# Key copy of the second pair on GpSimd, its lower part behind the key matches, and its query matches in another PSUM bank

## The chip, the cores and the metric

One core of one Trainium2 chip runs the whole program. The metric is the device time of one execution in microseconds (us), as the median of several runs. The core has TensorE (PE; its weight loads are listed as PEld), VectorE (DVE), ScalarE (ACT), GpSimd (POOL) and SyncE (SP), which here only issues DMAs. Each engine works through its own instructions in a fixed order.

## What is computed

Attention with a hash mask, followed by two feed-forward layers. Each query and key row gets a 6-bit bucket from the signs of its products with `proj`; a query sees only the keys of its own bucket.

```python
mask = q_bucket[:, :, :, None] == k_bucket[:, :, None, :]
scores = np.where(mask, scale * np.matmul(q, k.transpose(0, 1, 3, 2)), -1e9)
attn_out = softmax(scores) @ v                       # 2 batches, 8 heads, 768 rows, 64 wide
x = rearranged attn_out                              # 1536 tokens x 512
x = np.maximum(x @ w_in, 0) ** 2 @ w_out             # layer one, 2048 wide
h = x @ w_in2
return (np.maximum(h, 0) + alpha * np.minimum(h, 0)) @ w_out2   # layer two
```

All results are f32. The kernel gets f32 quality out of TensorE's f32r products by splitting a number into a high part (rounded to f32r) and a low part (the rest) and multiplying the parts.

## The kernel before

The 1536 tokens are cut into four chunks of 384 query rows. `attention_first` computes the attention of the first chunk with nothing beside it. After that `feed_forward` runs layer one for chunk after chunk, with the attention of the next chunk woven in, and then comes layer two.

In a chunk the eight heads are taken as four pairs, `Pair(c, j)`. In this text **pair 0** is `Pair(0, 0)`, **pair 1** is `Pair(0, 1)` (the one that the change touches), and so on. A pair has six **units**: head h = 0 or 1, and three blocks of 128 query rows. Units are counted on over the pairs of the first chunk: units 0 to 5 are pair 0 (3 to 5 its second head), 6 to 11 pair 1, 12 to 17 pair 2.

One unit does this: four products into a PSUM tile of two banks (`scores`, L468; the tiles `s` and `acc` take turns), the row maximum on VectorE (`low`, L476), the exponential on ScalarE (`sm`, L477, which frees the tile), then two units later two groups of three transposes on TensorE (`p_t`, L495, into a bank `m` or `x`) and an eviction of each group by ScalarE or VectorE (`pt`, L500 or L502, by the letters of `EVICT`). Later the products with the values follow (`blocks`, L512, into the bank `h`).

The operands of a unit's four products are stacked: 64 partitions hold the head's own numbers, the other 64 hold the bucket codes and the low parts. For keys, a pair needs in SBUF `kh`, the key rounded to f32r (`k_split`, L327, ScalarE), its low part (L328, VectorE, in place in `kr`), and the code matches (`k_ids`: products with `code`, L306, then L340 on VectorE). Four DMAs of 384 KB each then put them into `k`: for each head one from `kh` (`k_rows`, L334) and one from `kr` (L345). For queries: `q_ids` makes the matches (L314) and `q_yes` turns them into codes on ScalarE (L389, two instructions); `q_halves` makes high and low parts (L369 ScalarE, L370 GpSimd, L371 VectorE).

Pair 0 has its own preparation, `at_once`. For its second head one DMA of 96 KB copies a high part across partitions, `q<-q` (L433); the second of the four products of unit 3 is the first that waits for it, as the program's waits show.

What sets the order. Instructions that are passed to `tc.keep_in_program_order` keep the order in which the code is written; in the first chunk that holds for all of TensorE's and part of the others. The rest is placed by a list scheduler. SyncE's DMAs all go into one hardware queue, in the order in which the scheduler put them. PSUM banks: two for `m`, one `x` (every third `m_tile()`), one `h`, and two pairs for `s` and `acc`. The matches of pair 1's queries take an `m_tile()`, and the bank is free again when `q_yes` has read it.

Of the kernel before, what the change touches and what calls it, by code (L numbers as in the profile page):

```python
# [8 lines left out]
F32R = mybir.dt.float32r  # L9
# [3 lines left out]
AF = mybir.ActivationFunctionType  # L13
ALU = mybir.AluOpType
# [17 lines left out]
def kernel(  # L32
# [20 lines left out]
    nc = tc.nc  # L53
# [49 lines left out]
    def s_tile():  # L103

        state["s"] += 1
        if not state["moe"] and state["s"] % 2 == 0:
            return ps_a.tile([P, 2, 512], F32, tag="acc", name="acc")
        return ps_s.tile([P, 2, 512], F32, tag="s", name="s")

    def m_tile():  # L110

        state["m"] += 1
        if not state["moe"] and state["m"] % 3 == 0:
            return ps_a.tile([P, 512], F32, tag="x", name="x")
        return ps_m.tile([P, 512], F32, tag="m", name="m")

    def h_tile():

        state["h"] += 1
        if not state["attention"] and state["h"] % 3:  # L120
            return ps_m.tile([P, 512], F32, tag="m", name="m")
        return ps_h.tile([P, 512], F32, tag="h", name="h")

    def f32(ap):
        return ap.bitcast(F32)
# [89 lines left out]
    def load_values(b, j):  # L215
        vr = p4.tile([P, NKB, 2 * D], F32, tag="vr", name="vr")
        keys[b, j][-1] = vr
        return nc.sync.dma_start(out=vr, in_=v[b, j])

    class Pair:  # L220
# [78 lines left out]
        def matches(self, bits, n):  # L299

            w = n // NG
            if n > T and self.c == 0 and not self.first:
                halves = [m_tile()[:, 0:T] for _ in range(2)]
                for g in range(NG):
                    a, k = divmod(g * w, T)
                    self.pe(nc.tensor.matmul(halves[a][:, k:k + w], code[:, g, :], bits, start=True, stop=True))  # L306
                return halves
            if n > T:
                ps = s_tile()
            else:  # L310
                ps = m_tile().unsqueeze(1)
            for g in range(NG):
                a, k = divmod(g * w, T)
                self.pe(nc.tensor.matmul(ps[:, a, k:k + w], code[:, g, :], bits, start=True, stop=True))  # L314
            return ps[:, 0:n // T, 0:T]
# [8 lines left out]
        def k_split(self):  # L324
            self.new_k()
            kh = p1.tile([P, S], F32R, tag="kh", name="kh")
            self.next(nc.scalar.activation(kh, self.kr[:, 1], AF.Copy))  # L327
            nc.vector.tensor_tensor(self.kr[:, 1].bitcast(F32R), self.kr[:, 1], f32(kh), ALU.subtract)  # L328
            self.kh = kh
            self.k_rows(0)  # L330

        def k_rows(self, h):
            r, o = self.rows(h)
            nc.sync.dma_start(out=f32(self.k[r, h]), in_=f32(self.kh[r]).unsqueeze(1).to_broadcast([D, 2, S]))  # L334

        def k_ids(self):
            y = self.matches(self.k_code, S)
            ids = self.kr[:, 0].bitcast(F32R).rearrange("p (a n) -> p a n", n=T)
            for x, to in [(y[a], ids[:, a]) for a in range(2)] if self.c == 0 else [(y, ids)]:
                nc.vector.tensor_scalar(to, x, pop, -1.0, ALU.not_equal, ALU.mult)  # L340
            for h in range(2):
                r, o = self.rows(h)
                if h:
                    self.k_rows(1)
                ins = nc.sync.dma_start(out=f32(self.k[o, h]), in_=self.kr[r])  # L345
            keyed[self.c, self.j] = ins

            tc.keep_in_program_order(load_values(self.b, self.j))
            self.vr = keys[self.b, self.j][-1]
# [960 lines left out]
```

## Time and profile before

| what | us |
|---|---|
| median of 3 runs | 770.59 (770.19 to 771.94) |
| the profiled execution, its own time | 770.93 |
| its span, first to last instruction | 769.2 |
| time of that execution outside the span | 1.7 |

The profile is one execution. Times in the rows are microseconds from the start of the span. "[1.85 <-ACT q L389]" behind a row says that the engine had been idle for 1.85 us before it, and that the ScalarE instruction of line 389 ended the idle time. A row's second number runs to the end of its last instruction; the next row can start before that, since the engines are pipelined. The granted clock of TensorE is 1.00 of full speed in every row used here.

### The profile page before, as it was taken

Reading aid. Unit: us, or ns where it says so; the run is one execution under the profiler, and the core shown is the slowest. Engines: PE = TensorE matmul, PEld = TensorE weight load, DVE = VectorE, ACT = ScalarE, POOL = GpSimd, SP = SyncE. Lnnn points to the kernel's source line nnn. Section 1 sums busy time; section 2 is a strip of 40 time slices with the busy share of each in tenths; the row PEclk is TensorE's granted clock in tenths of the full one; section 3 lists DMA queues with packets and bytes.
Section 4 is the critical chain, followed back from the end, with each engine's and each line's share of the span. In section 5 each row is a group of like instructions: output and inputs, shape, how many; then the busy total and the mean of one; then the engine's idle time right before and its main releaser. Section 6 shows DMA issues by size and latency. Waiting matters only on the chain. (4 is left out here: it accounts for less than half of the span.)

```text
span 769.2 us, 12401 instructions
## 1 busy us (share of the span) xinstructions
PE 750.9 (98%) x4361; PEld 636.2 (83%) x4361; DVE 536.9 (70%) x950; ACT 510.0 (66%) x990; POOL 141.7 (18%) x89
## 2 busy tenths in 40 slices
PE   7999999999999999999999999999999999999998
PEld 4667877877887878778778789999998889998886
DVE  8878888887886969998888654836665914665111
ACT  8987887876665757767666567757786435876331
POOL 1101000000000000000000000006566535567440
PEclk9999999999999999999999999999999999999999
DMA  6778877978888997788866685332212246311222
GB/s 182 201 189 278 257 239 259 281 224 234 229 265 242 262 267 257 261 302 270 265 237 196 206 278 179 110 117 97 95 52 60 66 139 225 108 66 55 68 56 95
DMA packets 56705, 143.65 MB, mean 187 GB/s; under 512 B 7402, under 2 KB 11652, under 8 KB 56644
## 3 DMA queue, kind: packets, MB, share of 16 engines
q1 hardware_dynamic: 56644, 142.87, 59.6%
q8 instruction: 34, 0.56, 0.3%
q14 instruction: 27, 0.22, 0.1%
HBM read 96.62 MB, written 25.47 MB: 159 GB/s over the span
## 5 line engine op out<-in xcount | busy, mean ns | idle before, releaser
L1028 POOL TENSOR_TENSOR wp<-wraw,wp 128x1024 fp32r<-128x1024 f32 (+1 forms) x30 | 63.7, 2126 | 499.3 <-ACT wp L1025 486.4
L766 DVE TENSOR_TENSOR wl<-wf,wh 128x512 fp32r<-128x512 f32 x128 | 86.6, 686 | 17.8 <-ACT wh L765 17.3
L477 ACT ACTIVATE sm<-s,low 128x768 f32<-128x768 f32 x84 | 75.5, 898 | 28.9 <-DVE low L476 28.8
L765 ACT ACTIVATE wh<-wf 128x512 fp32r<-128x512 f32 x128 | 79.2, 627 | 20.8 <-DMA wf<-w 6.8
L476 DVE TENSOR_REDUCE low<-s 128x1 f32<-128x768 f32 x84 | 80.2, 954 | 16.3 <-PE s L468 15.2
L495 PE MATMUL m<-ident,sm 128*128 128x128 f32 x531 | 82.5, 274 | 2.6 <-ACT q L389 1.8
L468 PE MATMUL s<-k,q 128*128 128x384 f32 x336 | 76.9, 350 | 4.1 <-ACT sm L477 3.9
L495 PEld LDWEIGHTS m<-ident,sm 128*128 128x128 f32 x531 | 65.0, 140 | 18.0 <-ACT q L389 2.1
L1125 PE MATMUL b<-wp,gp 128*128 128x512 f32 x192 | 75.1, 391 | 0.0
L803 PE MATMUL h<-xh,wh 128*128 128x384 f32 x208 | 74.4, 358 | 0.6 <-ACT u L518 0.3
L999 PE MATMUL b<-xph,wp 128*128 128x384 f32 x224 | 74.9, 334 | 0.0
L1000 PE MATMUL b<-xpl,wp 128*128 128x384 f32 x224 | 74.9, 334 | 0.0
L1001 PE MATMUL b<-xph,wp 128*128 128x384 f32 x224 | 74.9, 334 | 0.0
L1126 PE MATMUL b<-wp,gp 128*128 128x512 f32 x192 | 74.8, 390 | 0.0
L1115 POOL TENSOR_TENSOR gp<-g,gp 128x768 fp32r<-128x768 f32 x32 | 62.4, 1954 | 51.3 <-ACT gp L1112 51.2
L468 PEld LDWEIGHTS s<-k,q 128*128 128x128 f32 x336 | 56.9, 188 | 17.7 <-ACT sm L477 11.3
L804 PE MATMUL h<-xl,wh 128*128 128x384 f32 x208 | 70.7, 340 | 0.0
L805 PE MATMUL h<-xh,wl 128*128 128x384 f32 x208 | 70.4, 338 | 0.0
L1109 DVE TENSOR_TENSOR wp<-wp 128x512 fp32r<-128x512 f32 x28 | 26.0, 938 | 62.4 <-ACT wp L1106 59.1
L844 PE MATMUL acc<-wh,gh 128*128 128x512 f32 x144 | 61.9, 431 | 0.0
L502 DVE COPY pt<-m 128x384 f32<-128x384 f32 x99 | 54.0, 550 | 7.1 <-PE m L495 6.8
L845 PE MATMUL acc<-wl,gh 128*128 128x512 f32 x144 | 57.4, 399 | 0.0
(191 smaller groups left out, 1647.7 us busy)
## 6 DMA issues: line engine op xcount, KB each, us to landing
wf<-w SPq DMA_DIRECT2D x96, 256.0 KB, 4.0
wbits<-in_w_in_dram SPq DMA_DIRECT2D x32, 512.0 KB, 4.7
wbits<-in_w_out_dram SPq DMA_DIRECT2D x32, 512.0 KB, 5.6
wraw<-ws SPq DMA_DIRECT2D x16, 896.0 KB, 4.6
q<-q SPq DMA_DIRECT2D x48, 192.0 KB, 4.5
w<-wf SPq DMA_DIRECT2D x32, 256.0 KB, 4.4
wp<-w SPq DMA_DIRECT2D x32, 256.0 KB, 2.6
k<-kh SPq DMA_DIRECT2D x14, 384.0 KB, 7.6
```

What stands on the lines that cost most here:

```text
L468: self.pe(nc.tensor.matmul(ps[:, a, 0:HALF], self.q[:, h, i, qs], self.k[:, h, i, ks], start=i == 0, stop=i == 1))
L476: low_ins = nc.vector.tensor_reduce(low, ps[:, 0:2, 0:HALF], AX.XY, ALU.max, negate=True)
L477: sm_ins = nc.scalar.activation(sm.rearrange("p (a n) -> p a n", a=2), ps[:, 0:2, 0:HALF], AF.Exp, bias=low, accum_out=self.sums[:, i:i + 1],)
L495: self.pe(nc.tensor.transpose(ps[:, i * P:(i + 1) * P], pp[:, b * P:(b + 1) * P], ident))
L765: nc.scalar.activation(hi, w, AF.Copy)
L766: nc.vector.tensor_tensor(lo, w, f32(hi), ALU.subtract)
L803: nc.tensor.matmul(hp, wih[:, ks], xh[:, kk, :], start=first, stop=False)
L999: nc.tensor.matmul(ps, w[0][:, ms], gh, start=first, stop=False, skip_group_check=True)
L1000: nc.tensor.matmul(ps, w[0][:, ms], gl, start=False, stop=False, skip_group_check=True)
L1001: nc.tensor.matmul(ps, w[1][:, ms], gh, start=False, stop=last, skip_group_check=True)
L1125: nc.tensor.matmul(a, g[:, 0, b], w[:, 0], start=f == 0, stop=False)
L1126: nc.tensor.matmul(a, g[:, 0, b], w[:, 1], start=False, stop=False)
```

## The change

Four edits, all in the first chunk. (1) `kh` of pair 1 is copied by GpSimd and no longer by ScalarE. (2) The subtraction that makes the key's low part is a method of its own, `k_low`, and for pair 1 it is written behind the two L340 instructions of `k_ids`. (3) The query matches of pair 1 go to the bank `h` and not to an `m_tile()`; the count of `m_tile()` calls is one lower from there on, so which of the later tiles is `m` and which is `x` shifts. (4) `kh` of pairs 2 and 3 is kept in program order on ScalarE.

```diff
-                ps = m_tile().unsqueeze(1)
+                ps = (h_tile() if (self.c, self.j) == (0, 1) else m_tile()).unsqueeze(1)
...
             kh = p1.tile([P, S], F32R, tag="kh", name="kh")
-            self.next(nc.scalar.activation(kh, self.kr[:, 1], AF.Copy))
-            nc.vector.tensor_tensor(self.kr[:, 1].bitcast(F32R), self.kr[:, 1], f32(kh), ALU.subtract)
             self.kh = kh
+            if (self.c, self.j) == (0, 1):
+                tc.keep_in_program_order(nc.gpsimd.tensor_copy(kh, self.kr[:, 1]))
+            else:
+                ins = nc.scalar.activation(kh, self.kr[:, 1], AF.Copy)
+                if self.c == 0:
+                    tc.keep_in_program_order(ins)
+                self.k_low()
             self.k_rows(0)
+
+        def k_low(self):
+            nc.vector.tensor_tensor(self.kr[:, 1].bitcast(F32R), self.kr[:, 1], f32(self.kh), ALU.subtract)
...
                 nc.vector.tensor_scalar(to, x, pop, -1.0, ALU.not_equal, ALU.mult)
+            if (self.c, self.j) == (0, 1):
+                self.k_low()
```

Line numbers of the changed kernel are 4 to 10 higher from here on. The scheduler also places other things anew. Below are three places in the two programs, with buffer numbers.

SyncE's queue, from the first DMA that pair 0's preparation issues; `kh_255` and `k_254` are pair 1's, `kr_216` its raw keys, `kr_229` and `qn_231` the loads for pair 2, `q_175` pair 0's queries. Before:

```order
L403 DMA k_174<-k_174 64x768
L200 DMA kr_229<-in_kT_dram 128x768
L433 DMA q_175<-q_175 64x384
L206 DMA qn_231<-in_qT_dram 128x384
L334 DMA k_254<-kh_255 64x2x768
L345 DMA k_254<-kr_216 64x1536
L334 DMA k_254<-kh_255 64x2x768
L345 DMA k_254<-kr_216 64x1536
```

And in the changed kernel:

```order
L413 DMA k_174<-k_174 64x768
L342 DMA k_254<-kh_255 64x2x768 x2
L200 DMA kr_229<-in_kT_dram 128x768
L443 DMA q_175<-q_175 64x384
L206 DMA qn_231<-in_qT_dram 128x384
L355 DMA k_254<-kr_216 64x1536 x2
```

Both DMAs from `kh_255` now stand ahead of the loads for pair 2 and of `q_175<-q_175`.

ScalarE, from behind the exponential of unit 1 (`sm_278`, `sm_306`, `sm_331` are units 2, 3 and 4; `m_290` and `m_295` or `x_295` are the transposes of unit 0, `m_320` the second group of unit 1, `q_286` is pair 1's). Before:

```order
L327 ACTIVATE kh_255<-kr_216 128x768
L500 ACTIVATE pt_289<-m_290 128x384
L500 ACTIVATE pt_289<-x_295 128x384
L477 ACTIVATE sm_278,sums_173<-acc_272,low_277 128x768
L389 ACTIVATE q_286<-m_281,off_114 64x384 x2
L477 ACTIVATE sm_306,sums_173<-s_300,low_305 128x768
L369 ACTIVATE q_286<-qn_218 64x384 x2
L500 ACTIVATE pt_289<-m_320 128x384
L500 ACTIVATE pt_289<-x_334 128x384
```

And in the changed kernel:

```order
L510 ACTIVATE pt_289<-m_290 128x384
L510 ACTIVATE pt_289<-m_295 128x384
L510 ACTIVATE pt_289<-m_320 128x384
L487 ACTIVATE sm_278,sums_173<-acc_272,low_277 128x768
L399 ACTIVATE q_286<-h_281,off_114 64x384 x2
L487 ACTIVATE sm_306,sums_173<-s_300,low_305 128x768
L379 ACTIVATE q_286<-qn_218 64x384 x2
L487 ACTIVATE sm_331,sums_173<-acc_325,low_330 128x768
L510 ACTIVATE pt_289<-m_334 128x384
```

The key copy is gone, and the eviction of unit 1's second group has moved ahead of the exponential of unit 2.

TensorE, from the last product of pair 1's query matches (tile 281) on. Before:

```order
L314 MATMUL m_281<-bits_243,code_111 128x96
L495 MATMUL m_290<-ident_108,sm_226 128x128 x3
L495 MATMUL x_295<-ident_108,sm_226 128x128 x3
L468 MATMUL s_300<-k_174,q_175 128x384 x4
L495 MATMUL m_315<-ident_108,sm_251 128x128 x3
L495 MATMUL m_320<-ident_108,sm_251 128x128 x3
L468 MATMUL acc_325<-k_174,q_175 128x384 x4
```

And in the changed kernel:

```order
L314 MATMUL h_281<-bits_243,code_111 128x96
L505 MATMUL m_290<-ident_108,sm_226 128x128 x3
L505 MATMUL m_295<-ident_108,sm_226 128x128 x3
L478 MATMUL s_300<-k_174,q_175 128x384 x4
L505 MATMUL x_315<-ident_108,sm_251 128x128 x3
L505 MATMUL m_320<-ident_108,sm_251 128x128 x3
L478 MATMUL acc_325<-k_174,q_175 128x384 x4
```

The sequence is the same; the banks differ. Unit 3 (`s_300`) stands ahead of both groups of unit 1 in both programs. Further down the queue, the loads of two weight blocks (`wbits`, 512 KB each), which stood behind all of pair 3's key rows, now stand ahead of pair 2's.

## Rows read from the trace of the kernel before

**Rows 1.** Busy time by stretch: window, its length, then us per engine, clock, DMA

```profile
10.00:18.00 8.00, 5.98 (x42) 4.80 (x41) 6.11 (x9) 7.41 (x15) 0.46 (x1) 1.00 0.64 157
24.00:36.00 12.00, 11.91 (x85) 8.18 (x86) 10.39 (x19) 10.58 (x24) 1.61 (x2) 1.00 0.83 207
36.00:60.00 24.00, 23.60 (x170) 17.28 (x171) 19.06 (x32) 20.80 (x45) 1.69 (x2) 1.00 0.66 184
```

**Rows 2.** Timeline of TensorE: start, us, what; units 3, 6, 9, 12, transposes

```profile
13.00 0.94 PE L468 MATMUL s<-k,q 128*128 128x384 f32 x4
...
16.11 0.55 PE L495 MATMUL m<-ident,sm 128*128 128x128 f32 x3 [1.85 <-ACT q L389]
...
19.99 0.97 PE L468 MATMUL acc<-k,q 128*128 128x384 f32 x4 [0.47 <-ACT sm L477]
...
25.80 0.49 PE L495 MATMUL x<-ident,sm 128*128 128x128 f32 x3
26.20 0.96 PE L468 MATMUL s<-k,q 128*128 128x384 f32 x4
...
35.04 0.94 PE L468 MATMUL acc<-k,q 128*128 128x384 f32 x4
```

**Rows 3.** Timeline of ScalarE from the key copy to the exponential of unit 7

```profile
12.39 0.83 ACT L327 ACTIVATE kh<-kr 128x768 fp32r<-128x768 f32 x1
...
13.49 0.49 ACT L500 ACTIVATE pt<-x 128x384 f32<-128x384 f32 x1
13.86 0.91 ACT L477 ACTIVATE sm<-acc,low 128x768 f32<-128x768 f32 x1
...
14.89 1.17 ACT L389 ACTIVATE q<-m,off 64x384 fp32r<-64x384 f32 x2
16.08 0.90 ACT L477 ACTIVATE sm<-s,low 128x768 f32<-128x768 f32 x1
...
16.97 1.05 ACT L369 ACTIVATE q<-qn 64x384 fp32r<-64x384 f32 x2
...
18.94 0.90 ACT L477 ACTIVATE sm<-acc,low 128x768 f32<-128x768 f32 x1
...
25.16 0.89 ACT L477 ACTIVATE sm<-s,low 128x768 f32<-128x768 f32 x1
```

**Rows 4.** Timeline of SyncE's DMA issues: start, us that the issue took

```profile
3.57 0.44 SPq L200 DMA_DIRECT2D kr<-in_kT_dram  x1
...
8.81 0.47 SPq L433 DMA_DIRECT2D q<-q  x1
9.39 0.53 SPq L206 DMA_DIRECT2D qn<-in_qT_dram  x1
13.25 0.66 SPq L334 DMA_DIRECT2D k<-kh  x1
...
25.29 0.62 SPq L334 DMA_DIRECT2D k<-kh  x1
```

**Rows 5.** GpSimd: two casts of the timeline, and a group of the page

```profile
4.78 0.82 POOL L402 CAST k<-k 64x768 fp32r<-64x768 f32 x1 [3.44 <-ACT k L401]
6.26 0.67 POOL L405 CAST q<-q 64x384 fp32r<-64x384 f32 x1 [0.67 <-ACT q L404]
...
L1115 POOL TENSOR_TENSOR gp<-g,gp 128x768 fp32r<-128x768 f32 x32 | 62.4, 1954 | 51.3 <-ACT gp L1112 51.2
```

**Rows 6.** Stretches again; the last two numbers are DMA share and GB/s

```profile
12.00:13.00 1.00, 1.00 (x12) 0.67 (x9) 1.00 (x3) 1.00 (x3) 0.00 (x0) 1.00 0.09 29
14.00:15.00 1.00, 0.26 (x3) 0.02 (x1) 1.00 (x2) 0.98 (x3) 0.00 (x0) 1.00 0.42 89
14.50:24.20 9.70, 7.31 (x60) 6.03 (x61) 7.53 (x12) 9.48 (x22) 2.40 (x4) 1.00 0.94 221
```

**Rows 7.** DMA issues of the first 10 us: KB, then us from issue to landing

```profile
qn<-in_qT_dram SPq DMA_DIRECT2D x3, 192.0 KB, 3.5
vr<-in_v_dram SPq DMA_DIRECT2D x1, 384.0 KB, 4.4
```

## The prediction

> **What bounds the kernel now.** I read the stretches first, then TensorE's timeline where it is idle, then the timelines of the engines that end that idle time, and last SyncE's issues and the DMA table. The stretches [rows 1] show two regimes. From 24 to 36 us TensorE is busy 11.91 of 12.00 us, and from 36 to 60 us 23.60 of 24.00: whatever TensorE has lost by 24 us, it can make up less than half a microsecond of before 60. From 10 to 18 us it is busy 5.98 of 8.00, while ScalarE is busy 7.41: here TensorE waits and ScalarE sets the pace. The largest idle time of that stretch is one row [rows 2]: the transposes at 16.11 us had 1.85 us of idle time ahead of them, ended by L389, `q_yes`. These transposes (second group of unit 1) wanted the bank that held pair 1's query matches, and `q_yes` stood in ScalarE's row behind the key copy, two evictions and an exponential [rows 3]. The change aims at this place, so the question is how early TensorE reaches unit 9 (26.20 us before [rows 2]), from where its row is full. A shift there is a shift of the end.
>
> **The change, part by part.** *Removed.* The key copy leaves ScalarE: 0.83 us at 12.39 us [rows 3]. The bank wait goes, 1.85 us on TensorE [rows 2], because the matches now sit in `h`, which the order shows unused until the values' products. If nothing else were late, TensorE would gain at most these 1.85 us.
>
> *Added on GpSimd.* One cast of 128x768. The trace has no such cast; below it is 64x768 in 0.82 us, above it 128x768 with two inputs in 1.95 us [rows 5]. I take 0.82, the same operation of the same length per partition. It starts when pair 1's raw keys have landed. They were issued at 3.57 us [rows 4]; a load of the same size landed 4.4 us after its issue [rows 7], so at 8.0. The copy ends at about 8.9.
>
> *Moved on SyncE.* This is the part that decides. Both DMAs from `kh`, 384 KB each, now stand in SyncE's row ahead of the key load for pair 2 (384 KB) and of `q<-q` (96 KB), and they wait for GpSimd. Before, `q<-q` was issued at 8.81 us [rows 4] and had landed by 12.9, since the query load issued behind it at 9.39 landed 3.5 us later [rows 4, 7]; unit 3, which needs it, ran at 13.00 without any wait [rows 2]. Now the first `kh` DMA is issued at 9.0, the second 0.66 later [rows 4], the load after that, and `q<-q` at about 10.9. Its bytes stand behind 1152 KB. The bytes of a DMA into an empty queue begin about 1.3 us after the issue: the one issued at 13.25 [rows 4] gives the second from 14 to 15 a DMA share of 0.42 [rows 6], so from 14.6 on. That puts the first bytes at 10.3. The full queue moved 221 GB/s from 14.5 to 24.2 us, mostly with these same copies [rows 6]: 1248 KB are 1.28 MB, 5.8 us, to 16.1. Landing comes some 0.8 us after the bytes: the load that landed at 12.9 left only a share of 0.09 in the second from 12 to 13 [rows 6], so its bytes were over at 12.1. **`q<-q` lands at 16.9 us**, and unit 3's second product waits for it, where it ran at 13.2 before.
>
> *What is queued behind that wait.* TensorE keeps its order, so both transpose groups of unit 1 wait with unit 3. On ScalarE the eviction of the second group now stands ahead of the exponential of unit 2, so ScalarE stops too. From the landing: three products, 0.6 us until the next group can start; one group later the second starts, 0.40 us (25.80 to 26.20 [rows 2]), and ends 0.49 later: 18.4. ScalarE evicts (0.37 until the next, 13.49 to 13.86 [rows 3]): 18.8. Exponential of unit 2, 1.03 (13.86 to 14.89): 19.8. `q_yes`, 1.19 (14.89 to 16.08): 21.0. Exponential of unit 3, 0.89 (16.08 to 16.97): 21.9. The two L369, 1.05: 22.9. Exponential of unit 4 at 22.9, against 18.94 before [rows 3]. It frees the tile for unit 6 after 0.9 us, as before (19.99, idle time ended by `sm` [rows 2]): unit 6 at 23.9, 3.9 us late. From unit 4's to unit 7's exponential ScalarE needed 6.22 us (18.94 to 25.16 [rows 3]); it now has one eviction more in between and 0.2 us of idle time less, so the shift stays at 3.9 to 4.1 up to unit 9. Written as a rule: the shift is the landing of `q<-q` minus 12.9.
>
> *Beside it at no cost.* `k_low` now precedes the maximum of unit 2 on VectorE: 0.9 us later for a maximum that ScalarE asks for at 18.8, so the wait hides it; without the wait it would cost ScalarE most of that. Pair 1's own key rows: two of four DMAs are early, the other two follow `q<-q` and the query load, 1.0 MB more, 4.5 us at 221 GB/s, landing at about 21, ahead of unit 6 at 23.9. The two weight loads of 512 KB ahead of pair 2's key rows are 4.7 us of queue. Before, pair 2's first key row was issued at 25.29 and its first unit ran at 35.04 [rows 2, 4], 9.7 us later, and needs 768 KB, 1.3 + 3.6 + 0.8 = 5.7 us. So 4.0 us are free, and the loads start before the rows, which wait for ScalarE. I take 0, and 0.7 as the upper end. The kept order of `kh` for pairs 2 and 3 and the shifted bank names change places in a row where TensorE is full: 0, within 0.5 either way.
>
> *Sum.* Landing 16.9 minus 12.9 gives 4.0, less 0.1 for the little slack up to 60 us: +3.9 us on the profiled execution's 770.93 is 774.8. The median of the runs is 0.34 below that execution, so 770.59 + 3.9 = 774.5 us.
>
> **Rivals.** *A: the bank wait goes and nothing comes in its place.* If `q<-q` still landed by 12.9, TensorE would lose no time at unit 3, and up to 1.85 us would be won: 768.7. For it speaks that ScalarE has one copy less in a stretch where it is the bound [rows 1]. Against it, `q<-q` is issued behind a DMA that cannot be issued before 9.0; it decides the other way only if 96 KB land within 2 us of an issue at 10.9, and the shortest landing in [rows 7] is 3.5.
>
> *B: only the later issue counts.* If the 16 DMA engines let the small transfer end with little regard to the copies ahead of it, it lands 3.5 us after its issue [rows 7]: 14.4, and the shift is 1.5: 772.1, at the border of what counts as no change. For it: its bytes are a thirteenth of the queue's. Against it: the DMA share is 0.94 over ten microseconds of such copies [rows 6], so a later transfer finds no idle engine. The Trainium skill ("DMA: Bandwidth & Descriptors", Anatomy of one DMA) gives 2.0 us plus the bytes at 436 GB/s for one DMA, on another issue path; by that the landing would be an estimated 13.9 and the time 771.6. The trace does not agree: 221 GB/s in a full queue [rows 6].
>
> *C: GpSimd is slow.* At 1.95 us [rows 5] the copy ends at 10.0 and everything behind is 1.1 later: 775.6, and with 0.7 for the weight loads 776.3. For it: the half as long 64x384 cast took 0.67 against 0.82 [rows 5], so a cast can be slower than its length says. The Trainium skill ("SBUF — State Buffer", Who interferes with whom) has GpSimd and a VectorE instruction with two SBUF inputs block each other entirely, and pair 0's preparation has such subtractions on VectorE at that time; no row here settles it.
>
> That the change does not do what it says is out: the order shows each of the moves.
>
> **How the numbers follow.** Forecast 0.66 at 774.5; A 0.07 at 768.7; B 0.14 at 772.1, of which I put 0.08 within no change; C 0.13 at 775.6 to 776.3. What can be told from no change here is about 0.2%, 1.5 us, so the borders are 769.1 and 772.1. Faster 0.07; within 0.2% 0.09, which is B's part and a little for a forecast that later idle time eats; slower 0.84. The forecast's own bounds are a landing between 15.5 and 17.9 us, +2.6 to +5.0, 773.2 to 775.6. The range reaches to B below, 771.9, and to C above, 776.3; it leaves out A and the tails.
>
> **What would show it.** In the profile of the changed kernel: a gap of 3 us or more in TensorE's row in the middle of unit 3, ended by a DMA `q<-q`; SyncE's row with two `k<-kh` issues from about 9.0 on and `q<-q` behind them near 11; ScalarE idle from about 13.7 to 18 in front of its third eviction; no wait for L399 any more; unit 6 at about 23.9 and unit 9 at about 30. I am wrong if unit 3 runs near 13 without a wait, which makes A true, or if the wait is there but unit 12 is no later than about 36, which would mean that the full row had slack after all.

## The result

The changed kernel takes 774.82 us (median of 22 runs) beside 771.23 us for the kernel before (22 runs in the same session): ratio 1.0053, with a 95% interval from 1.0034 to 1.0071. A second set of runs of the same file gave 775.50 us, ratio 1.0076 (1.0048 to 1.0105). It is slower by about half a per cent, near the forecast of 774.5 us. The profiled execution took 773.33 us, 1.5 us less than the median of its runs; its span is 771.5.

**Stretches** of the changed kernel, in the columns of [rows 1]: window, its length, busy time of TensorE, weight load, VectorE, ScalarE, GpSimd, then granted clock, DMA share and GB/s.

```profile
10.00:18.00 8.00, 5.45 (x41) 4.21 (x41) 5.32 (x8) 3.16 (x7) 0.00 (x0) 1.00 0.86 212
24.00:36.00 12.00, 11.08 (x87) 7.99 (x87) 11.02 (x19) 10.87 (x23) 1.51 (x3) 1.00 0.71 197
21.00:22.00 1.00, 1.00 (x4) 1.00 (x5) 0.00 (x0) 0.96 (x3) 0.00 (x0) 0.50 0.91 289
22.00:23.00 1.00, 1.00 (x6) 0.90 (x5) 0.50 (x1) 1.00 (x3) 0.00 (x0) 0.50 0.09 26
```

From 10 to 18 us ScalarE is busy 3.16 us where it was busy 7.41 [rows 1]: it no longer sets the pace there, it stands still. TensorE is not faster for that, 5.45 us against 5.98. From 24 to 36 us TensorE has 0.92 us of idle time, where it had 0.09: the full row of [rows 1] begins later. The last two rows hold something that [rows 1] has nowhere: a granted clock of 0.50, the 1.2 GHz level, while TensorE is full again.

**SyncE's issues**, which answer [rows 4], and the new cast on GpSimd. The two stretches behind them show when the bytes begin: the DMA share is the last number but one.

```profile
9.69 1.30 SPq L342 DMA_DIRECT2D k<-kh  x2
11.09 1.43 SPq L200 DMA_DIRECT2D kr<-in_kT_dram  x1
12.62 1.58 SPq L443 DMA_DIRECT2D q<-q  x1
```

```profile
8.84 0.82 POOL L329 CAST kh<-kr 128x768 fp32r<-128x768 f32 x1 [1.92 <-DMA kr<-in_kT_dram]
```

```profile
10.00:11.00 1.00, 1.00 (x17) 0.60 (x16) 0.96 (x2) 0.30 (x1) 0.00 (x0) 1.00 0.01 3
11.00:12.00 1.00, 1.00 (x11) 0.88 (x4) 0.52 (x2) 0.90 (x2) 0.00 (x0) 1.00 0.95 194
```

The order is the one that was read from the code: both copies from `kh`, the key load of pair 2, then `q<-q`. GpSimd's cast took the 0.82 us that were taken for it, but the raw keys landed only when it started, at 8.8 us instead of 8.0.

**TensorE**, which answers [rows 2]: units 3, 4, 6, 9 and 12 (start, duration, in brackets the idle time ahead and what ended it).

```profile
14.89 0.42 PE L478 MATMUL s<-k,q 128*128 128x384 f32 x1
17.86 0.77 PE L478 MATMUL s<-k,q 128*128 128x384 f32 x3 [2.55 <-DMA q<-q]
...
20.75 1.65 PE L478 MATMUL acc<-k,q 128*128 128x384 f32 x4 [1.46 <-ACT sm L487]
...
25.31 0.55 PE L505 MATMUL m<-ident,sm 128*128 128x128 f32 x3 [0.48 <-ACT pt L510]
25.61 0.95 PE L478 MATMUL acc<-k,q 128*128 128x384 f32 x4
...
31.95 0.97 PE L478 MATMUL s<-k,q 128*128 128x384 f32 x4
...
40.80 0.95 PE L478 MATMUL acc<-k,q 128*128 128x384 f32 x4
```

The first product of unit 3 runs, then 2.55 us pass until `q<-q` is there. The wait for L389 of [rows 2] is gone, and no wait for L399, which took its place, has come.

**ScalarE**, which answers [rows 3]:

```profile
14.84 0.87 ACT L510 ACTIVATE pt<-m 128x384 f32<-128x384 f32 x2
19.32 0.49 ACT L510 ACTIVATE pt<-m 128x384 f32<-128x384 f32 x1 [3.61 <-PE m L505]
19.71 0.90 ACT L487 ACTIVATE sm<-acc,low 128x768 f32<-128x768 f32 x1
...
20.72 1.16 ACT L399 ACTIVATE q<-h,off 64x384 fp32r<-64x384 f32 x2
21.91 0.90 ACT L487 ACTIVATE sm<-s,low 128x768 f32<-128x768 f32 x1
...
23.88 0.90 ACT L487 ACTIVATE sm<-acc,low 128x768 f32<-128x768 f32 x1
```

It stands idle for 3.61 us in front of its third eviction, and then needs 4.56 us from there to the exponential of unit 4 (19.32 to 23.88), much as the prediction's chain had it (18.4 to 22.9).

### The profile page after: what moved, and what is told of

Its sections match the earlier page's. It is cut to its first block, busy times and chain, and to the rows that moved or that the text cites. A ratio compares the mean times of both kernels' runs of the same rounds, so it can differ in the third digit from the quotient of the medians.

```text
span 771.5 us, 12403 instructions
## 1 busy us (share of the span) xinstructions
PE 753.7 (98%) x4361; PEld 639.0 (83%) x4361; DVE 537.5 (70%) x950; ACT 507.6 (66%) x989; POOL 142.5 (18%) x90
## 4 chain that ended last, share of the span: by engine, by line
PE 87%; DMA 6%; DVE 3%; ACT 3%; issue 1%; SPq 1%; ACTq 0%; DVEq 0%
PE s L478 7%; PE m L505 6%; PE b L1135 6%; PE b L1136 6%; PE m L522 5%; PE b L1141 5%; PE b L1011 5%; PE b L1010 5%; PE b L1009 5%; PE h L813 4%; PE h L814 4%; PE h L815 4%; PE acc L858 4%; PE acc L855 3%; PE acc L854 3%; PE h L522 2%
## 5 line engine op out<-in xcount | busy, mean ns | idle before, releaser
L478 PE MATMUL s<-k,q 128*128 128x384 f32 x336 | 78.5, 354 | 5.8 <-DMA q<-q 2.5
```

Of the source, the lines that this page charges most:

```text
L478: self.pe(nc.tensor.matmul(ps[:, a, 0:HALF], self.q[:, h, i, qs], self.k[:, h, i, ks], start=i == 0, stop=i == 1))
```

## A second look at both kernels

By the two first profiles, unit 6 is 5.62 us late (25.61 against 19.99 [rows 2]), while the spans are only 2.4 apart (771.5 and 769.2). So I first believed that layer one gives some 3 us back. To test that, both kernels were run again, without an edit.

> The changed kernel as it is, on the same chip as the three others. Ratio 1.0034 to 1.0071 as in its first comparison. In its trace: unit 3's wait ended by q<-q between 15.5 and 17.9 us, unit 6 at 23.9 to 25.6. It also tells whether the 3.4 us at half clock behind that wait, and the late rise of the clock to full speed at 13.6 us, come again.

Measured: 775.50 us, ratio 1.0076, a little above the expected range; unit 3's second product at 17.28 us, 3.00 us of idle time ahead, unit 6 at 25.35, span 771.6. Stretches at a granted clock of 0.50 came again, in other places: from 8.12 to 11.53 us and from 18.36 to 25.19.

> The kernel before, unchanged: a second profiled execution of it, and a measure of how far a comparison of a kernel with itself strays. All theories: ratio 1.000 with an interval that holds 1.000; a stretch at half clock of under 4 us in all; unit 6 within 0.5 us of 20, layer one's first product within 1 us of 71.7. Open: whether the time from layer one's first product to the end is 697.5 us again, as in the first profile. Theory 1 (the changed kernel gives 2 to 3 us back behind layer one's start): 697 to 698. Rival (that time varies from run to run, and the first profile of before was a long one): 693 to 696.

Measured: 771.38 us, ratio 1.0003 (0.9986 to 1.0019), so a comparison of a kernel with itself strays by up to 0.19%. Unit 6 and layer one's first product came 2.3 us later than in the first profile, which no theory expected. TensorE in this second profile of the kernel before, the first unit to be compared, then units 3, 4, 6 and 12:

```profile
8.43 1.65 PE L468 MATMUL acc<-k,q 128*128 128x384 f32 x4 [0.66 <-ACT q L422]
...
15.31 0.95 PE L468 MATMUL s<-k,q 128*128 128x384 f32 x4
...
18.42 0.55 PE L495 MATMUL m<-ident,sm 128*128 128x128 f32 x3 [1.84 <-ACT q L389]
...
22.31 0.97 PE L468 MATMUL acc<-k,q 128*128 128x384 f32 x4 [0.47 <-ACT sm L477]
...
37.36 0.94 PE L468 MATMUL acc<-k,q 128*128 128x384 f32 x4
...
74.00 0.44 PE L803 MATMUL h<-xh,wh 128*128 128x384 f32 x1 [0.35 <-ACT u L518]
```

The same first unit in the first profile of before, and layer one's first product in the changed kernel:

```profile
7.90 0.96 PE L468 MATMUL acc<-k,q 128*128 128x384 f32 x4 [0.66 <-ACT q L422]
```

```profile
77.10 0.45 PE L813 MATMUL h<-xh,wh 128*128 128x384 f32 x1 [0.35 <-ACT u L528]
```

In the second profile unit 0's four products took 1.65 us; in the first they took 0.96, the duration of units 3 to 12 in [rows 2]. So one and the same kernel begins with its products at either pace; the changed kernel's first profile has 1.65 us too. The pace is that of TensorE's clock. The packed trace of the first profile of before has its first clock record (a level with its start and length), a granted 1.00, at 5.84 us; that of the second has it at 13.56, and that of the changed kernel at 13.58. In the last two, the products of units 0 and 1 ahead of it take 1.65 us, which is what four such products take at a recorded 0.50 (20.75 us of the changed kernel). The stretches of a profile show 1.00 where no record has begun, so a slow beginning can stay unseen in them.

**Comparing like with like**, the changed kernel (first profile) stands against this one: unit 6 +3.30 us (25.61 to 22.31), unit 12 +3.44 (40.80 to 37.36), layer one's first product +3.10 (77.10 to 74.00), the span +3.5 (771.5 to 768.0). The shift arises before unit 6 and passes to the end. In this pair nothing is given back: the time from layer one's first product to the end is 694.4 us in one and 694.0 in the other. What misled me was the first profile of before: it had the quick start, and later more waits (697.5 us from the same place to the end). Of these, one wait is seen when the waits of TensorE between 320 and 520 us are listed, here for the first profile of before and for the first of the changed kernel:

```profile
PE m L937 <- DMA wf<-w: 1.6, 1, 1.6
```

```profile
PE m L947 <- DMA wf<-w: 1.8, 1, 1.8
```

A weight load comes late in both. The second profile of the changed kernel has 1.0 us of this wait, the second of before has none. So 694.4 and 694.0 are alike in sum and not in their waits. In the fourteen profiled executions of all the kernels here, the time from layer one's first product to the end goes from 691.0 to 697.5 us. That is more than the shift in question, so what shows that layer one does not give it back is the medians, 3.6 and 4.6 us apart, and not one pair of profiles.

## Is it the place of the query copy in the queue?

The theory is the prediction's: `q<-q` behind two copies from `kh` and a load. The rival is that the cost lies in the other moves (cast on GpSimd, lower part later, ScalarE's new order) and that the late transfer is only what the trace shows.

**Undo the queue order alone.** In the changed kernel, the DMAs from `kh` are held behind `q<-q`:

```
-            nc.sync.dma_start(out=f32(self.k[r, h]), in_=f32(self.kh[r]).unsqueeze(1).to_broadcast([D, 2, S]))
+            ins = nc.sync.dma_start(out=f32(self.k[r, h]), in_=f32(self.kh[r]).unsqueeze(1).to_broadcast([D, 2, S]))
+            if (self.c, self.j) == (0, 1):
+                behind(ins, state["qq"])
...
-            nc.sync.dma_start(out=f32(q[o[1], 1, 1]), in_=f32(q[r[1], 1, 0]))
+            state["qq"] = nc.sync.dma_start(out=f32(q[o[1], 1, 1]), in_=f32(q[r[1], 1, 0]))
```

> The changed kernel with one thing more: SyncE issues q<-q (and the load for pair 2) ahead of both DMAs from kh. All else stays: GpSimd's copy, the bank, the moved subtraction, the later order of ScalarE and TensorE. Queue theory: unit 3 runs without a DMA wait, unit 6 at 19 to 20.0 us (19.99 in the kernel before, 25.61 in the changed one), and the time is that of the kernel before or up to 1.9 us below it, ratio 0.997 to 1.001. Rival (the loss comes from the other moves, banks and scheduler): unit 6 stays late and the ratio stays near 1.005.

Measured: 771.58 us, ratio 1.0008 (0.9985 to 1.003). `q<-q` is issued at 8.98 us. TensorE at units 3, 4 and 6, and ScalarE's third eviction:

```profile
13.48 0.97 PE L480 MATMUL s<-k,q 128*128 128x384 f32 x4
...
16.57 0.96 PE L480 MATMUL acc<-k,q 128*128 128x384 f32 x4 [1.46 <-ACT sm L489]
...
21.44 0.93 PE L480 MATMUL acc<-k,q 128*128 128x384 f32 x4
```

```profile
15.14 0.49 ACT L512 ACTIVATE pt<-m 128x384 f32<-128x384 f32 x1 [0.95 <-PE m L507]
```

The wait at unit 3 is gone, and with it the loss. This carries the main verdict. Two things belong beside it. The profiled execution, 768.32 us, is the shortest of its twelve and began at the quick pace. Counted from the first product of unit 3, which takes that out, unit 6 follows after 7.96 us; in the changed kernel's two profiles it follows after 10.72 and 11.51, in the two of before after 6.99 and 7.00. And the other moves are kept up to 58 us only: so far the traces show the changed kernel's order on TensorE, ScalarE and VectorE. Behind that the scheduler has placed a large part of ScalarE's and VectorE's work in layer one anew. The time from layer one's first product (72.12 us) to the end is 694.2 us, beside 694.4 and 694.9 in the changed kernel, so in these executions the gain lies ahead of it. Unit 6 is at 21.44 us, not at the 19 to 20 that were expected: what is left is 0.95 us of idle time on ScalarE, of which more below.

**Half the dose.** The same edit for the second copy alone (`(self.c, self.j, h) == (0, 1, 1)`), so that one copy of 384 KB stays ahead of `q<-q`:

> The changed kernel with q<-q issued between the two DMAs from kh: one copy of 384 KB stands ahead of it and not two. Queue theory, as a dose: one copy less is 384 KB at 221 GB/s, 1.8 us, so q<-q lands at 15.9 us where the changed kernel shows 17.7 (unit 3's wait ends at 17.86), unit 6 comes 1.8 us earlier than in the changed kernel, 23.8, and the ratio falls to about 1.002 to 1.004. Rival (it is the issue time alone that counts): nearly no change against the changed kernel, since q<-q is issued only 0.7 us earlier. Rival (other moves): ratio near 1.005.

Measured: 773.83 us, ratio 1.0036 (1.0012 to 1.0059). This is the purest of the edits: on ScalarE and VectorE the trace shows the changed kernel's order from the first instruction to the last. The time is between the two, as expected, but its interval holds the changed kernel's 1.0053 and overlaps that of the first experiment, so the time alone does not prove the dose. The landing shows it: 16.26 us, 6.6 us behind the first issue from `kh` (9.70), where the changed kernel's landings came 8.0 and 8.1 us behind it. Unit 6 is not earlier than in the changed kernel, and the profiled execution, 769.64 us, is the shortest of its twelve:

```profile
16.39 1.30 PE L480 MATMUL s<-k,q 128*128 128x384 f32 x3 [2.97 <-DMA q<-q]
...
25.58 1.18 PE L480 MATMUL acc<-k,q 128*128 128x384 f32 x4
```

```profile
19.01 0.49 ACT L512 ACTIVATE pt<-m 128x384 f32<-128x384 f32 x1 [5.32 <-PE m L507]
```

```profile
18.00:21.00 3.00, 1.54 (x7) 1.14 (x6) 1.15 (x2) 1.95 (x5) 0.00 (x0) 0.50 0.99 212
21.00:24.00 3.00, 3.00 (x13) 2.90 (x12) 1.55 (x3) 2.92 (x6) 0.81 (x2) 0.50 0.47 119
```

In this execution TensorE ran at the lower clock level from the wait on until 26 us (0.50 from 15.85 to 26.09), so the way from unit 3's second product to unit 6 took 9.19 us; in the changed kernel, with a shorter stretch at that level, it took 7.75 (17.86 to 25.61).

**The same delay put into the kernel before.** Two extra copies of 384 KB to a scratch tile, ahead of `q<-q`; nothing else of the change:

```
+            spare = dram.tile([P, 2, S], F32, tag="spare", name="spare")
+            for a in range(2):
+                ins = nc.sync.dma_start(
+                    out=spare[a * D:(a + 1) * D], in_=f32(k[o[1], 1, 1]).unsqueeze(1).to_broadcast([D, 2, S])
+                )
+                behind(state["late"], ins)
```

> The kernel before, with nothing of the change, but with two extra transfers of 384 KB each on SyncE ahead of q<-q (a copy of key rows to a scratch tile that nobody reads). Theory (the place of q<-q behind 768 KB in the queue is the cause, wherever it comes from): q<-q lands about 3.4 us later than before, near 16.3 us; unit 3's second product waits some 3 us for it, where the kernel before has no wait; unit 6 is 2 to 5 us later than 19.99 us, the ratio 1.002 to 1.005. Rival 1 (the cost comes from the new order of ScalarE's and VectorE's work, which this kernel hardly has): a wait at unit 3, but unit 6 within 1 us of the kernel before, ratio within 1.000 +- 0.0015. Rival 2 (the queue lets a small transfer pass): no wait at unit 3, ratio 1.000.

Measured: 774.43 us, ratio 1.0041 (1.0022 to 1.0059), but the landing came at 14.8 us, not 16.3. My figure was wrong: I had added the two copies' time to the old landing, although they were issued at 8.35 us and their bytes began soon after. Unit 3 waited 0.96 us. The profiled execution was the shortest of all of this kernel's, so it was run again:

> The same kernel as q_late, for a second profiled execution: the first one was the shortest of its 12 runs. Theory (the place in the queue costs it the time): q<-q lands at 14.5 to 15.5 us again, unit 3 waits about 1 us for it, and unit 6 or layer one's first product is 2 to 4 us late. Rival (the extra bytes disturb later transfers, the wait at unit 3 is not what costs): wait at unit 3 under 1 us, later waits for transfers between 24 and 60 us, layer one's first product later by 3 us or more than unit 6 is.

Measured: 772.45 us, ratio 1.0017 (1.0001 to 1.0033). The landing is again at 14.9 us, but this execution began at the slower pace, unit 3 started at 15.30 and did not wait at all. In both, TensorE waited 1.1 us near 26 us for `bits` of pair 2, whose raw keys stand behind the extra copies, and that brings unit 12 to 39.03 us, 1.67 later than in the second profile of before. So this pair comes nearer to its rival: the wait at unit 3 is under 1 us and a wait for late bytes comes behind it, though layer one's first product is only 0.8 us later than unit 6 is (1.68 and 0.91 us against the second profile of before), where the rival had 3. A cost is there, but of another kind, and the edit also changes ScalarE's order from 16 us on. As a proof that lateness of `q<-q` alone suffices it failed.

## Is it the bank, the idle ScalarE, or the clock?

**The bank alone.** The kernel before with the query matches in `h`, and nothing else of the change:

```
-                ps = m_tile().unsqueeze(1)
+                ps = (h_tile() if (self.c, self.j) == (0, 1) else m_tile()).unsqueeze(1)
```

> The kernel before with only the bank changed: pair 1's query matches go to the bank h. ScalarE keeps the key copy, SyncE its order. Expected: q<-q lands as before, unit 3 at 13.0 without a wait, and the 1.85 us of idle time ended by L389 are gone. If TensorE is what waits, unit 6 comes up to 1.8 us earlier (18.2) and the ratio is 0.9975. If ScalarE is the bound of that stretch, as its 7.41 of 8.00 busy us say, unit 6 stays within 0.5 us of 19.99 and the ratio within 0.999 to 1.001.

Measured: 770.64 us, ratio 0.9998 (0.998 to 1.0017). The 1.85 us of [rows 2] are gone, and nothing is gained: unit 6 follows 7.79 us behind unit 3 (15.19 to 22.98), in the kernel before 7.0. The scheduler's order on ScalarE changes with the bank, from 13.5 us on. TensorE behind the place, at units 4, 5 and 6:

```profile
16.96 0.97 PE L468 MATMUL acc<-k,q 128*128 128x384 f32 x4 [0.18 <-ACT sm L477]
...
19.17 0.97 PE L468 MATMUL s<-k,q 128*128 128x384 f32 x4 [0.58 <-ACT sm L477]
20.64 0.55 PE L495 MATMUL m<-ident,sm 128*128 128x128 f32 x3 [0.50 <-ACT pt L500]
22.04 0.55 PE L495 MATMUL m<-ident,sm 128*128 128x128 f32 x3 [0.85 <-ACT pt L500]
22.98 0.94 PE L468 MATMUL acc<-k,q 128*128 128x384 f32 x4 [0.39 <-DMA k<-kr]
```

Five waits, 2.50 us in sum, four of them for ScalarE, stand where the kernel before has two, 1.85 and 0.47 us [rows 2]. [rows 1] had said why: ScalarE was busy 7.41 of 8.00 us there. A wait for a bank went; the engine that empties the banks was no faster.

**ScalarE's standstill.** In the changed kernel, the eviction that waits for TensorE is put behind the exponential of unit 2, so that ScalarE works during the wait:

```
+            if (self.c, self.j, h, t, a) == (0, 0, 0, 1, 1):
+                behind(ins, scored[0, 0, 2][1])
```

> The changed kernel, with one move on ScalarE: the eviction of unit 1's second group stands behind the exponential of unit 2 instead of ahead of it, so that ScalarE can do that exponential and L399 while TensorE waits for q<-q. q<-q lands as late as in the changed kernel, near 17.5 us. Theory (the landing is passed on at full size because ScalarE's row stands still behind the eviction): ScalarE does 2.2 us of its row during the wait, and unit 6 comes 1.5 to 2.2 us earlier than 25.5 us, ratio 1.002 to 1.005. Rival (the shift is TensorE's own waiting time, whatever ScalarE does): unit 6 within 0.5 us of 25.5 us, ratio 1.005 to 1.0076.

Measured: 773.59 us, ratio 1.0039 (1.0021 to 1.0058). ScalarE during the wait, then TensorE at units 3 and 6:

```profile
15.95 0.90 ACT L487 ACTIVATE sm<-acc,low 128x768 f32<-128x768 f32 x1 [0.91 <-DVE low L486]
...
16.97 1.16 ACT L399 ACTIVATE q<-h,off 64x384 fp32r<-64x384 f32 x2
```

```profile
18.55 0.77 PE L478 MATMUL s<-k,q 128*128 128x384 f32 x3 [3.92 <-DMA q<-q]
...
24.63 0.94 PE L478 MATMUL acc<-k,q 128*128 128x384 f32 x4
```

From unit 3's second product to unit 6 it now takes 6.08 us instead of 7.75: 1.7 us of ScalarE's work lie inside the wait. In this execution the transfer was later, so unit 6 itself gains 1.0 us only, where 1.5 to 2.2 were expected, and the ratio fell by an amount that its interval does not separate from the changed kernel's. The mechanism is seen in the trace; its worth in the time is not settled.

**The clock.** Eight products of constant data into unit 3's tile, ahead of its own, to keep TensorE at work while it waits. A second edit holds the exponential of unit 2 behind the eviction of unit 1's second group, the order that the changed kernel has:

```
+            if (self.c, self.j, h, t) == (0, 0, 1, 0):
+                for _ in range(8):
+                    self.pe(nc.tensor.matmul(ps[:, 0, :], blank[:, 0:P], blank, start=True, stop=True))
...
+            if (self.c, self.j, h, t, a) == (0, 0, 0, 1, 1):
+                behind(scored[0, 0, 2][1], ins)
```

> The changed kernel with eight products of constant data (some 1.7 us) put into unit 3's tile ahead of its own products, where TensorE otherwise waits for q<-q; what is computed is the same. Theory 1 (the half-clock stretch behind the wait is a cost of its own): the wait for q<-q shrinks to under 1.2 us, the landing stays near 17.5 us, no stretch at half clock after 18 us, and unit 6 comes 1 to 2 us earlier than in the changed kernel (25.4 to 25.6 us): ratio to the kernel before 1.003 to 1.005 where the changed kernel has 1.005 to 1.0076. Rival (the clock costs nothing there, since ScalarE sets the pace behind the landing): unit 6 within 0.4 us of 25.5, same ratio as the changed kernel.

Measured: 775.08 us, ratio 1.0051 (1.0029 to 1.0072). The wait shrank to 0.35 us, and the clock fell all the same, at 20.09 us, behind the other wait, which the products could not fill:

```profile
17.27 0.76 PE L481 MATMUL s<-k,q 128*128 128x384 f32 x3 [0.35 <-DMA q<-q]
...
20.15 1.65 PE L481 MATMUL acc<-k,q 128*128 128x384 f32 x4 [1.46 <-ACT sm L490]
...
25.02 0.94 PE L481 MATMUL acc<-k,q 128*128 128x384 f32 x4
```

From 17.27 to 25.02 are 7.75 us, to the hundredth what the changed kernel takes. That TensorE idles in front of the landing costs nothing beyond the landing. What the lower clock costs behind it, this run did not tell, since it was not taken away. The traces of the other runs do. From ScalarE's third eviction to unit 6 the changed kernel takes 6.29 us (19.32 to 25.61), with the granted clock at 0.50 from 20.41 to 23.82. The kernel with `q<-q` first takes 6.30 us (15.14 to 21.44) at 1.00, and the half dose 6.57 us (19.01 to 25.58) at 0.50 throughout. So on this part ScalarE's row sets the time, and the lower clock costs 0.3 us at most. Ahead of it, from unit 3's second product to that eviction, ScalarE waits for TensorE's transposes: 1.46 us at 1.00 (17.86 to 19.32) and 2.62 at 0.50 (16.39 to 19.01). These 1.2 us are most of the difference between the half dose and the changed kernel (9.19 and 7.75).

The list of runs leaves one thing open. Of the changed kernel's 22 executions, the four with a mean granted clock of 0.996 or more took 771.55 to 773.33 us, the twelve at 0.993 took 772.10 to 775.97, and the six below that 775.17 to 780.97. Its executions have 0.993 and 0.994 on the average of either set, those of the kernel before 0.997 to 0.999. So part of the 3.6 us between the medians goes with more time at 0.50, behind waits that the change brings or elsewhere; the profiled executions do not show where.

## What the lower part on VectorE costs, and a kernel that is faster than both

With `q<-q` early, ScalarE still waited 0.95 us. The reason was in the prediction: `k_low` stands ahead of the maximum of unit 2 on VectorE, and the wait that hid it is gone. So the next kernel takes the queue order of the first experiment, puts `k_low` behind that maximum, and the eviction behind the exponential:

```
+            if (self.c, self.j, i) == (0, 0, 2):
+                behind(state["klow"], low_ins)
```

> The changed kernel with q<-q and pair 2's key load issued ahead of both DMAs from kh (as in q_first), the eviction of unit 1's second group behind unit 2's exponential, and the lower part of the keys behind unit 2's maximum on VectorE. A try at a kernel that keeps what the change removes from ScalarE and pays none of its costs. Theory: q<-q lands by 13, no wait at unit 3, unit 6 at 19.5 to 20.5 us, no stretch at half clock behind it, ratio 0.997 to 1.000. Rival (ScalarE's freed 0.83 us brings nothing because the row is full by 24 us in any case, or because pair 1's own key rows are now late): unit 6 at 20.5 to 22 us, or a wait at unit 6 for k, ratio 1.000 to 1.003.

Measured: 767.97 us, ratio 0.9968 (0.9949 to 0.9987); `q<-q` landed at 12.8 us, no wait at unit 3, unit 6 at 20.46. The profiled execution, 770.62 us, is the longest of its twelve. It was repeated without the edit on the eviction, which the order of `k_low` brings about by itself:

> The changed kernel with q<-q and pair 2's key load ahead of both DMAs from kh, and the lower part of the keys behind unit 2's maximum. The order of the instructions on every engine comes out the same as in best, so this is best a second time, in a shorter edit. Theory (best's gain is real): ratio 0.995 to 0.999, no wait at unit 3. Rival (a lucky set of runs): 0.999 to 1.002.

Measured: 767.65 us, ratio 0.9966 (0.9947 to 0.9985). And with the eviction's edit, but with `k_low` where the changed kernel has it:

> The changed kernel with q<-q and pair 2's key load ahead of both DMAs from kh, and the eviction of unit 1's second group behind unit 2's exponential on ScalarE, but the lower part of the keys ahead of unit 2's maximum on VectorE as in the changed kernel. With best2 it tells what that place on VectorE costs. Theory (ScalarE waits 0.9 us for unit 2's maximum, which stands behind the lower part): idle time of some 0.9 us ahead of unit 2's exponential, unit 6 some 0.9 us later than in best2, ratio 0.9985 to 1.001. Rival (the maximum is hidden): no idle time there, ratio within 0.001 of best2.

Measured: 770.80 us, ratio 1.0001 (0.9982 to 1.002). ScalarE's exponential of unit 2 in this kernel, then in the faster one:

```profile
15.95 0.90 ACT L491 ACTIVATE sm<-acc,low 128x768 f32<-128x768 f32 x1 [1.16 <-DVE low L490]
```

```profile
14.82 0.90 ACT L491 ACTIVATE sm<-acc,low 128x768 f32<-128x768 f32 x1 [0.28 <-DVE low L490]
```

The idle time is 0.9 us longer, as expected, and unit 6 comes 0.8 us later (22.37 against 21.58), or 0.5 when counted from the start of unit 2. The times differ by 3.1 us (770.80 to 767.65). So the trace accounts for less than a third of it here.

Nor does unit 6 say why these two kernels beat the kernel before: counted from the start of unit 2, which takes the pace of the beginning out, unit 6 follows after 8.97 and 9.56 us, in the two profiles of before after 8.95 and 9.16. That leaves layer one, where the scheduler's order comes out another way with each of these edits. The profiles fit this without proving it: from layer one's first product to the end the repeated faster kernel takes 691.1 us and the kernel before 697.5 and 694.0, but the first faster kernel takes 695.3, and the half dose, which is no faster, 691.0. TensorE's waits between 200 and 320 us, in the second profile of before and then in the repeated faster kernel (us in total, times, longest):

```profile
PE m L314 <- DVE pt L502: 1.0, 1, 1.0
PE s L468 <- ACT sm L477: 1.0, 1, 1.0
PE m L495 <- DVE pt L502: 0.7, 1, 0.7
```

```profile
PE m L281 <- ACT pt L516: 0.2, 1, 0.2
```

The first profile of before has the same three waits, 2.6 us in sum, and a fourth of 0.6. That is the size of the gain, 2.6 us by the first ratio. But the kernel with `k_low` early, at ratio 1.0001, has only 0.7 us of waits there, and that of the first experiment, at 1.0008, has 2.9, so these waits alone do not sort the kernels. What makes `k_low`'s place worth 3 us stays open.

## Why the prediction was right

**The cause** was the one named: undoing the queue order takes the ratio from 1.0053 and 1.0076 to 1.0008 and unit 3's wait away. Half of it gives 1.0036, between the two, though not clear of either by its interval; the attempt to bring the loss into the kernel before by the queue alone failed. Rival A (only the bank wait goes) fell twice: the wait at unit 3 is there, and the bank wait is worth nothing by itself. Rival B (only the later issue counts) fell at the landing: the transfer came 17.7 us into the program, not 14.4. Rival C fell at the cast, 0.82 us.

**The sum, term by term.**
- Start of the cast: 8.84 us, taken as 8.0. The raw keys needed 5.2 us from issue to landing, not the 4.4 of [rows 7]. This is the largest miss in the landing. In the second profile the cast began at 8.17.
- Cast: 0.82, as taken.
- From the first issue of `kh` to the landing: taken as 7.9 us (9.0 to 16.9). By the two profiles, it is 8.0 (9.69 to 17.7) and 8.1 (9.02 to 17.1). The rule of 221 GB/s in a full queue [rows 6], 1.3 us ahead of the bytes and 0.8 behind, held to 0.2 us; the share of 0.95 from 11 us on shows the 1.3. The issue of `q<-q` itself was later than the 10.9 taken (12.62), without consequence, since the queue was full either way.
- Landing to the exponential of unit 4: taken as 6.0 us (16.9 to 22.9), measured from 17.7 to 23.88, 6.2.
- Exponential to unit 6: taken as 1.0 (22.9 to 23.9), measured as 1.73 (23.88 to 25.61). Unit 6 does not only wait for the tile here: the transposes ahead of it wait for an eviction that now stands behind the exponential (0.48 us at 25.31). The lower clock is not the reason: with `q<-q` first it is 1.73 us too (19.71 to 21.44), at 1.00.
- Unit 6 to unit 9: 6.34 us, against 6.21 of [rows 2]. As taken, the shift stays.
- The two weight loads ahead of pair 2's key rows: taken as 0. The shift is 3.44 us at unit 12 and 3.30 at unit 6, so 0.1 at most.
- `k_low`: taken as hidden by the wait, and as costing ScalarE most of 0.9 us without it. Both were seen: 0.95 us once the wait was undone.
- The shift to the end: taken as whole. Like with like it is: 3.30 us at unit 6, 3.5 at the span. By medians it is 3.6 and 4.6 us. The span's 3.5 is weaker than it looks, since layer one alone varies by more from execution to execution.

**Where the sum was lucky.** The rule "landing minus 12.9" assumes that unit 3 could start at 13.0 us, as [rows 2] has it. In the second profile of before it started at 15.31, in the changed kernel at 14.89. With the landing at 17.7, the rule would have given 4.8 us by the first, and some 2.5 by the second profile; the found 3.3 lies between, since the later landing, the late start and the 0.7 us at unit 6 work against each other. The step that was missing is that the place of unit 3 is not fixed: it depends on when TensorE's clock rises, 5.84 or 13.6 us in these profiles, and a profile shows a single execution, while the landing hangs on DMAs and does not move with the clock. Nor has the sum a term for the clock behind the wait; in the changed kernel's first profile it cost next to nothing, by the list of runs it may have cost something in others. That the forecast came within 0.4 us of the median is more than its working had earned; against the second set, 775.50 us, it is 1.0 off.

**GpSimd beside VectorE**, which Rival C left open. The cast on GpSimd was not slowed. But VectorE's instruction with two SBUF inputs that ran at 8.95 us took 1.12 us, where it took 0.55 in the kernel before (8.42 us), and 1.11 in the second profile of the changed kernel, beside the cast both times. That agrees with what the Trainium skill ("SBUF — State Buffer", Who interferes with whom) states: a VectorE instruction with two SBUF inputs contends with a GpSimd instruction that reads SBUF, and the order of issue decides which of the two blocks. In these traces the cast began first (8.84 us beside 8.95, and 8.17 beside 8.30), and VectorE is the one that waited. This loss lay beside a wait and cost nothing that these runs can tell.

## What to carry to other kernels

When an operation becomes ready earlier, look at what its transfers now stand ahead of in the queue: bytes that nobody needs for ten microseconds can hold up 96 KB that are needed at once. A wait that is removed from an engine gains only if the engine behind the wait has time; here ScalarE was full, and the bank wait was worth nothing. Take two profiles of the kernel before, and compare executions that began alike, before believing that a shift was given back. An edit of one line can let the scheduler order a whole layer anew; compare the orders in the two traces before saying that only one thing was changed.

## What the runs showed of the hardware

- The same first products took 0.96 us in some executions and 1.65 in others of the same kernel, and that moved unit 6 by 2.3 us (19.99 and 22.31). The clock record of a granted 1.00 begins at 5.84 us in the one and at 13.56 in the other. The spans, 769.2 and 768.0, do not show it, since the time behind layer one's first product varies by more (697.5 and 694.0).
- Issues on SyncE's queue took longer behind the copies from `kh`: `q<-q` 1.58 us and the key load 1.43, where [rows 4] have 0.47 for the same `q<-q` and 0.44 for such a load.
- Behind TensorE's waits of 2.5 to 3 us and 1.46 us, the granted clock fell to 0.50 with TensorE at work again: 20.41 to 23.82 us in the changed kernel, 18.36 to 25.19 in its second profile, 15.85 to 26.09 with the half dose. It is no sure sign of a loss: the faster kernel had such a stretch too, from 19.51 to 22.92 us, and where ScalarE's row set the time it cost nothing (6.29 us beside 6.30).
